# Where the float32 copies of attention's chunks are made: ScalarE against GpSimd

## The chip, the core and the metric

The kernel runs on one core of a Trainium2 chip, in one launch. The metric is the device time of that launch in microseconds (us). A core has five engines that run their own queues of instructions in order and wait for one another by semaphores: TensorE (PE in the profile, with its weight loads as PEld), VectorE (DVE), ScalarE (ACT), GpSimd (POOL) and SyncE (SP, which here only issues transfers).

## The reference, cut to what matters

Causal attention over 2 batches, 12 heads, 448 positions and a head size of 64, then two feed-forward blocks on its result `x` (896 tokens of 768 numbers), all in float32:

```
scores = where(mask, -1e9, q @ k.T / sqrt(64));  p = exp(scores - max) / (sum + 1e-9)
x  = (p @ v)                       # heads side by side: 896 x 768
x  = (x @ w_a * (x @ w_b)) @ w_out # 768 -> 1536 -> 768
h  = x @ w_in;  y = (h * sigmoid(h)) @ w_out2   # 768 -> 2048 -> 768
```

## The kernel before, in words

**Precision.** A float32 product is made of three products of a faster matmul type. Each operand is split: ScalarE (or GpSimd) casts it to a "hi" half, and VectorE subtracts the hi half from the operand to get the "lo" half; TensorE then adds hi·hi, hi·lo and lo·hi. The weights go through the same split in a longer conversion: two instructions on ScalarE (lines 205, 211) and two on VectorE (217, 222) for each of two loads, and then casts (244) and subtractions (248). One pair of weight loads is called a granule.

**Attention** runs over 12 units; a unit is one batch `b` and one chunk of two heads, with batch 0 in units 0 to 5 and batch 1 in units 6 to 11. A unit has four slots, and the program is written slot by slot, 61 slots in all. In a slot TensorE makes the scores of one group of query blocks (lines 552, 556), the transposes (`pt`, line 597) of a group that is 5 slots old, and the products with `v` (`xo`, line 614) of a unit that is 11 slots old. VectorE takes the scores with the mask and the row maxima (`sm`, 564), ScalarE the exponentials (`p`, 568) and the copies of most transposes out of their banks (`ptr`, 697); VectorE makes one `ptr` copy for each unit. The sums of the exponentials are inverted on VectorE (577, 578), and GpSimd multiplies the exponentials by that: the normalisations (581). GpSimd also makes the hi halves of the next unit's q and k (525). The transposes use two banks in turn, so a transpose waits until the copy of an earlier one has emptied its bank. Conversion of the first two granules is spread over slots 8 to 34 and 35 to 52.

**The end of a unit.** When `xo` of a unit is complete, `arrive` (from line 367) puts on ScalarE the cast `xh` (375) and right behind it a float32 copy `xf` (377), and on VectorE the subtraction `xl` (381). The halves are what the feed-forward's matmuls read. The float32 copies are read only by `sums_of` (from 383).

**The sums.** The fast products of the first feed-forward block (Strassen's form over 2 x 2 blocks) need sums and differences of chunks: for each of three pairs of chunks (`c` = 0, 1, 2) four additions `S` on VectorE (390), four casts on ScalarE (395, `p7h`, `p5h`, `p6h`, `p3h`) and four subtractions on VectorE (396). They are handed out one step a slot from slot 44 on, and behind attention one step every three matmuls. A pair can start when its last chunk of batch 1 has arrived: in slots 42, 50 and 58.

**Behind attention** TensorE goes through the granules one after another (line 287 records every such matmul). The first granule's products of batch 0 are mixed into the last slots of attention; the first granule to read the sums, and the first with the fast products, is the third, whose weight tiles are `wa`, `wb`, `wc` and `wd`.

Of the kernel before, what the change touches and what calls it, by code (L numbers as in the profile page):

```python
# [10 lines left out]
F32 = mybir.dt.float32  # L11
# [4 lines left out]
ALU = mybir.AluOpType  # L16
# [17 lines left out]
NQ = 3  # L34
SLOT_HI = 0
SLOT_LO = 2
SUMS0 = 44
SUMS_MM = 3
SPARE = 6
# [18 lines left out]
def fused_kernel(ctx: ExitStack, tc: tile.TileContext, qk, v, w_ab, w_mid, w_in, w_out, out):  # L58
# [14 lines left out]
    nc = tc.nc  # L73
# [45 lines left out]
    A = Ring(slots, [A1], (P, S))  # L119
# [249 lines left out]
    XS, XF = {}, {}  # L369

    def arrive(b, chunk, src):

        hi, lo = A.new(F32R, "xh"), A.new(F32R, "xl")
        XS[chunk, b] = hi, lo
        nc.scalar.copy(out=hi, in_=src)  # L375
        XF[chunk, b] = t = A.new(F32, "xf")
        nc.scalar.copy(out=t, in_=src)  # L377
        c, i = divmod(chunk, 2)
        if (b, i) != (1, 0):
            ACTS[{(0, 0): 1, (0, 1): 2, (1, 1): 4}[b, i]][c] = hi, lo  # L380
        return lambda: nc.vector.tensor_tensor(out=lo, in0=src, in1=hi[:].bitcast(F32), op=ALU.subtract)

    def sums_of(c):


        a11, a12, a21, a22 = (XF.pop((2 * c + i, b)) for b in range(B) for i in range(2))

        def add(name, a, b, op):
            t = A.new(F32, name)
            nc.vector.tensor_tensor(out=t, in0=a, in1=b, op=op)  # L390
            return t

        def halves_of(t, n):
            hi, lo = ACTS[n][c] = A.new(F32R, f"p{n}h"), A.new(F32R, f"p{n}l")
            nc.scalar.copy(out=hi, in_=t)
            return lambda: nc.vector.tensor_tensor(out=lo, in0=t, in1=hi[:].bitcast(F32), op=ALU.subtract)

        s3 = add("S", a11, a21, ALU.subtract)
        yield 2
        rest = halves_of(s3, 7)  # L400
        yield 1
        s1 = add("S", a21, a22, ALU.add)
        rest()
        A.free(a21, a22, s3)
        yield 2
        rest = halves_of(s1, 5)
        yield 1
        s2 = add("S", s1, a11, ALU.subtract)
        rest()
        A.free(s1, a11)  # L410
        yield 2
        rest = halves_of(s2, 6)
        yield 1
        s4 = add("S", a12, s2, ALU.subtract)
        rest()
        A.free(s2, a12)
        yield 2
        rest = halves_of(s4, 3)
        yield 0
        rest()  # L420
        A.free(s4)
# [21 lines left out]
    sums_x = Sums()  # L443
# [20 lines left out]
    with tc.manual_schedule():  # L464

        with ExitStack() as actx:
# [34 lines left out]
            late, now = {}, [0]  # L501
# [3 lines left out]
            def defer(k, prio, fn):  # L505
                late.setdefault(now[0] + k, []).append((prio, fn))
# [13 lines left out]
            def halves_hi(u):  # L520

                for n, src, shape in sources(u):
                    for e in "hl":
                        U[u][n + e] = h_p.tile(shape, F32R, tag=n + e, name=n + e)
                    nc.gpsimd.tensor_scalar(
                        out=U[u][n + "h"], in0=src, scalar1=1.0, scalar2=1.0, op0=ALU.mult, op1=ALU.mult)

            def halves_lo(u):
                for n, src, _ in sources(u):
                    nc.vector.tensor_tensor(  # L530
                        out=U[u][n + "l"], in0=src, in1=U[u][n + "h"].bitcast(F32), op=ALU.subtract)
# [41 lines left out]
            def normalize(u, groups):  # L573
                t = U[u]
                js = [j for i in groups for j in GROUPS[i]]
                cs = slice(COL[js[0]], COL[js[-1]] + 1)
                nc.vector.tensor_scalar_add(out=t["sums"][:, cs], in0=t["sums"][:, cs], scalar1=1e-9)
                nc.vector.reciprocal(out=t["rcp"][:, cs], in_=t["sums"][:, cs])
                for j in js:
                    pj = p_sb[u % 2][j][:, 0:D * (j + 1)]  # L580
                    nc.gpsimd.tensor_scalar(  # L581
                        out=pj, in0=pj, scalar1=t["rcp"][:, COL[j]:COL[j] + 1], scalar2=1.0,
                        op0=ALU.mult, op1=ALU.mult,
                    )
# [20 lines left out]
            def pv(u, kb):  # L605
                t = U[u]
                b, chunk = divmod(u, NP)
                if kb == 0:
                    pool, tag = ps_x, "x"
                    if u % 2:  # L610
                        pool, tag = ps_g[0], "g"
                    t["x"] = pool.tile([P, 512], F32, tag=tag, name="xo")
                for h in range(2):
                    nc.tensor.matmul(  # L614
                        out=t["x"][h * D:(h + 1) * D, kb * P:S], lhsT=t["v"][:, kb, h * D:(h + 1) * D],
                        rhs=t["pt"][:, kb, h, kb * P:S], start=(kb == 0), stop=(kb == NKB - 1),
                    )
                if kb == NKB - 1:
                    defer(1, 0, partial(finish, b, chunk, t["x"][:, 0:S]))
# [3 lines left out]
            def finish(b, chunk, src):  # L623
                tasks.append(arrive(b, chunk, src))
                if b == 1 and chunk % 2:
                    sums_x.gens.append(sums_of(chunk // 2))


            wz = const.tile([P, P], F32, name="wz")
# [38 lines left out]
            for s in range(n_slots):  # L668
# [10 lines left out]
                if i == SLOT_HI and u + 1 < NU:  # L679
                    halves_hi(u + 1)  # L680
                if i == SLOT_LO and u + 1 < NU:
                    halves_lo(u + 1)
# [18 lines left out]
                if 0 <= u < NU and i % 2 == 1:  # L701
                    normalize(u, (i - 1, i))
                if s >= SUMS0:
                    sums_x.step()
# [254 lines left out]
```

## Time and profile before

| what | value |
|---|---|
| three timed runs, median (lowest to highest) | 574.27 us (574.26 to 574.3) |
| the profiled execution's own time | 574.47 us |
| its span, from the first to the last instruction | 572.7 us |
| busy over the span: PE, DVE, ACT, POOL | 559.6, 422.1, 380.3, 72.4 us |
| granted TensorE clock over the span | 1.000 |

The profile is of one execution. What lies between its own time and its span (1.77 us) is outside the instructions. TensorE is busy for 98% of the span, so the places where it is not are few, and they are to be looked at one by one; the other engines' shares are means over stages with different limits.

### The profile page before, as it was taken

How to read it: one execution, taken by the hardware profiler on the slowest of the kernel's cores; microseconds unless marked ns; L12 is line 12 of the kernel's file. 1: busy time of each engine (PE TensorE's matmuls, PEld its weight loads, DVE VectorE, ACT ScalarE, POOL GpSimd, SP SyncE). 2: the span in 40 equal slices, each digit the busy share in tenths (PEclk: the TensorE clock that was granted, in tenths of full speed). 3: DMA queues.
4: the chain of work that ended last, by engine and by line, in shares of the span. 5: the costliest groups of instructions: out<-in, count | busy, mean ns of one | idle time of the engine just before them, and what ended most of it. 6: DMA issues, size and time to landing. Idle time of an engine off the chain costs nothing.

```text
span 572.7 us, 8396 instructions
## 1 busy us (share of the span) xinstructions
PE 559.6 (98%) x2978; PEld 490.4 (86%) x2978; DVE 422.1 (74%) x794; ACT 380.3 (66%) x754; POOL 72.4 (13%) x127
## 2 busy tenths in 40 slices
PE   8999997999999999999999999999999999999997
PEld 6666654799999999999999997899999999999996
DVE  6798897587989898969774769878887798342500
ACT  5989988675666666678654546888876896532601
POOL 6887764000000000000000000000000000000000
PEclk9999999999999999999999999999999999999999
DMA  7354423023333433333333332432324233531501
GB/s 246 115 183 131 121 69 136 1 111 110 111 110 118 160 127 143 116 111 110 112 110 111 110 111 69 152 112 110 111 92 140 81 106 117 169 131 60 175 0 64
DMA packets 18089, 65.41 MB, mean 114 GB/s; under 512 B 2176, under 2 KB 6784, under 8 KB 18048
## 3 DMA queue, kind: packets, MB, share of 16 engines
q1 hardware_dynamic: 18048, 64.89, 33.4%
q8 instruction: 23, 0.38, 0.3%
q14 instruction: 18, 0.15, 0.1%
HBM read 62.13 MB, written 2.75 MB: 113 GB/s over the span
## 4 chain that ended last, share of the span: by engine, by line
PE 89%; DVE 5%; ACT 3%; issue 1%; POOL 1%; DMA 1%; SPq 0%; POOLq 0%; ACTq 0%; DVEq 0%
PE acc L287 79%; PE pt L597 3%; PE xo L614 3%; PE sc L552 2%; PE sc L556 1%; DVE sm L564 1%; DVE wq L222 1%; POOL p L581 1%; ACT ptr L697 1%; DMA k<-qk 1%; ACT p L568 1%; DVE S L337 0%; ACT xf L377 0%; ACT xh L375 0%; DVE wq L217 0%
## 5 line engine op out<-in xcount | busy, mean ns | idle before, releaser
L217 DVE SCALAR_TENSOR_TENSOR wq<-wr 128x768 uint32<-128x768 uint32 (+1 forms) x76 | 66.5, 877 | 27.4 <-ACT wr L211 26.4
L310 ACT COPY s<-acc 128x448 f32<-128x448 f32 x72 | 38.4, 534 | 64.0 <-PE acc L287 63.5
L211 ACT ACTIVATE wr<-wr,wbias 128x768 uint32<-128x768 uint32 (+1 forms) x76 | 69.7, 917 | 0.0
L205 ACT ACTIVATE wr<-wr 128x768 f32<-128x768 f32 (+1 forms) x76 | 63.8, 839 | 3.8 <-DMA wr<-w_out 2.6
L222 DVE SCALAR_TENSOR_TENSOR wq<-wr,wq 128x768 uint32<-128x768 uint32 (+1 forms) x76 | 64.0, 873 | 0.0
L581 POOL TENSOR_SCALAR p<-p,rcp 128x448 f32<-128x448 f32 (+6 forms) x84 | 56.5, 690 | 21.1 <-ACT p L568 15.5
L568 ACT ACTIVATE p<-sm,nmax 128x448 f32<-128x448 f32 (+6 forms) x84 | 42.9, 522 | 10.4 <-DVE nmax L564 9.4
L287 PE MATMUL acc<-th,wgbl 128*128 128x448 f32 x168 | 49.5, 366 | 0.0
L287 PE MATMUL acc<-th,wgbh 128*128 128x448 f32 x168 | 49.4, 366 | 0.0
L287 PE MATMUL acc<-th,wgal 128*128 128x448 f32 x168 | 49.4, 365 | 0.0
L287 PE MATMUL acc<-tl,wgah 128*128 128x448 f32 x168 | 49.4, 366 | 0.0
L287 PE MATMUL acc<-tl,wgbh 128*128 128x448 f32 x168 | 49.4, 365 | 0.0
L287 PE MATMUL acc<-th,wgah 128*128 128x448 f32 x168 | 49.3, 365 | 0.0
L597 PEld LDWEIGHTS pt<-ident,p 128*128 128x128 f32 x192 | 20.2, 140 | 22.4 <-issue 10.8
L597 PE MATMUL pt<-ident,p 128*128 128x128 f32 x192 | 31.0, 285 | 5.5 <-ACT ptr L697 4.5
L564 DVE CUSTOM_DVE_ANT_0 sm<-sc,mask 128x448 f32<-128x448 f32 (+6 forms) x84 | 31.8, 411 | 4.5 <-PE sc L556 4.5
L287 PEld LDWEIGHTS acc<-th,wgbh 128*128 128x128 f32 x168 | 31.5, 188 | 2.9 <-DVE s L754 0.2
L287 PEld LDWEIGHTS acc<-th,wgah 128*128 128x128 f32 x168 | 31.5, 188 | 2.8
L287 PEld LDWEIGHTS acc<-th,wgal 128*128 128x128 f32 x168 | 31.6, 188 | 2.5
L287 PEld LDWEIGHTS acc<-th,wgbl 128*128 128x128 f32 x168 | 31.5, 188 | 2.5
L287 PEld LDWEIGHTS acc<-tl,wgbh 128*128 128x128 f32 x168 | 31.5, 188 | 2.5
L287 PEld LDWEIGHTS acc<-tl,wgah 128*128 128x128 f32 x168 | 31.5, 188 | 2.5
(167 smaller groups left out, 1384.6 us busy)
## 6 DMA issues: line engine op xcount, KB each, us to landing
wr<-w_ab SPq DMA_DIRECT2D x24, 768.0 KB, 5.2
wr<-w_in SPq DMA_DIRECT2D x16, 768.0 KB, 4.5
wr<-w_out SPq DMA_DIRECT2D x24, 512.0 KB, 4.1
wr<-w_mid SPq DMA_DIRECT2D x12, 768.0 KB, 4.5
v<-v SPq DMA_DIRECT2D x12, 256.0 KB, 4.1
q<-qk SPq DMA_DIRECT2D x24, 112.0 KB, 2.9
k<-qk SPq DMA_DIRECT2D x12, 224.0 KB, 3.5
out<-o SPq DMA_DIRECT2D x12, 224.0 KB, 3.9
```

Of the source, the lines that this page charges most:

```text
L205: nc.scalar.activation(out=word(i, 1).bitcast(F32), in_=word(i, 1).bitcast(F32), func=AF.Copy, scale=2.0 ** -112)
L211: nc.scalar.activation(out=word(i, 0), in_=word(i, 0), func=AF.Relu, bias=wbias, scale=2.0 ** -29)
L217: nc.vector.scalar_tensor_tensor(out=xi(i), in0=word(i, 1), scalar=3, in1=word(i, 0), op0=ALU.logical_shift_left, op1=ALU.bitwise_or)
L222: nc.vector.scalar_tensor_tensor(out=xi(i), in0=word(i, 1), scalar=0x80000000, in1=xi(i), op0=ALU.bitwise_and, op1=ALU.bitwise_or)
L287: nc.tensor.matmul(out=acc[:, 0:S], lhsT=w, rhs=a, start=first, stop=last, skip_group_check=True)
L310: nc.scalar.copy(out=t, in_=acc[:, 0:S])
L552: nc.tensor.matmul(out=sc, lhsT=t[a][:, j - BIG].rearrange("p h q -> p (h q)"), rhs=t[k][:, 0:K], start=(n == 0), stop=(n == 2))
L564: nc.vector.tensor_tensor_reduce(out=sm, in0=sc, in1=mask[:, S - K:S], op0=ALU.add, op1=ALU.min, scale=-(D ** -0.5), scalar=3.0e38, accum_ ...
L568: nc.scalar.activation(out=p_sb[u % 2][j][:, 0:K], in_=sm, func=AF.Exp, bias=t["nmax"][:, c:c + 1], scale=-1.0, accum_out=t["sums"][:, c:c ...
L581: nc.gpsimd.tensor_scalar(out=pj, in0=pj, scalar1=t["rcp"][:, COL[j]:COL[j] + 1], scalar2=1.0, op0=ALU.mult, op1=ALU.mult,)
L597: nc.tensor.transpose(out=pt[:, kb].rearrange("p h q -> p (h q)"), in_=p_sb[u % 2][j][:, kb * P:(kb + 1) * P], identity=ident,)
L614: nc.tensor.matmul(out=t["x"][h * D:(h + 1) * D, kb * P:S], lhsT=t["v"][:, kb, h * D:(h + 1) * D], rhs=t["pt"][:, kb, h, kb * P:S], start= ...
```

## The change

`arrive` no longer makes the copy `xf` on ScalarE. A new function `whole` makes it on GpSimd as the sum of the two halves. `finish` puts the four copies of a pair into a later slot: at least slot 49, which follows the last normalisation, and the slot after the pair's arrival where that is later; the pair's sums may start two slots behind that.

```
         hi, lo = A.new(F32R, "xh"), A.new(F32R, "xl")
         XS[chunk, b] = hi, lo
         nc.scalar.copy(out=hi, in_=src)
-        XF[chunk, b] = t = A.new(F32, "xf")
-        nc.scalar.copy(out=t, in_=src)
...
+    def whole(b, chunk):
+
+        hi, lo = XS[chunk, b]
+        XF[chunk, b] = t = A.new(F32, "xf")
+        nc.gpsimd.tensor_tensor(out=t, in0=hi[:].bitcast(F32), in1=lo[:].bitcast(F32), op=ALU.add)
...
             def finish(b, chunk, src):
                 tasks.append(arrive(b, chunk, src))
                 if b == 1 and chunk % 2:
-                    sums_x.gens.append(sums_of(chunk // 2))
+                    for n in range(4):
+                        put_off(partial(whole, n % 2, chunk - 1 + n // 2))
+                    put_off(lambda: sums_x.gens.append(sums_of(chunk // 2)), 2)
+
+            def put_off(fn, k=0):
+                defer(max(0, WHOLE - now[0]) + 1 + k, 9, fn)
```

`WHOLE` is 48. `defer(k, prio, fn)` runs `fn` k slots later. The order of the instructions on TensorE and of the transfers stays the same; it changes on ScalarE, VectorE and GpSimd. Line numbers behind the edit grow by up to 10.

On ScalarE, in the slots in which unit 11's exponentials are made, before:

```order
L568 ACTIVATE p_0_128,sums<-sm,nmax 128x64
L395 CAST p7h<-S 128x448
L244 CAST wgah<-wq 128x768
L375 CAST xh<-xo 128x448
L377 COPY xf<-xo 128x448
L697 COPY ptr<-pt 128x8x64
L568 ACTIVATE p_4_132,sums<-sm,nmax 128x320
```

And the same place with the change:

```order
L573 ACTIVATE p_0_128,sums<-sm,nmax 128x64
L245 CAST wgah<-wq 128x768
L376 CAST xh<-xo 128x448
L707 COPY ptr<-pt 128x8x64
L573 ACTIVATE p_4_132,sums<-sm,nmax 128x320
```

The copy `xf` is gone from in front of `ptr`, as it is in every unit, and the cast `p7h` of the first pair's sums has moved behind the exponentials.

On VectorE, from the last inversion of sums on, before (the numbers tell the buffers apart):

```order
L578 RECIPROCAL rcp_1348<-sums_1346 128x4
L390 TENSOR_TENSOR S_1474<-S_1430,xf_509 128x448
L396 TENSOR_TENSOR p5l_1455<-S_1430,p5h_1454 128x448
L248 TENSOR_TENSOR wgal_1400<-wq_1207,wgah_1399 128x768
L381 TENSOR_TENSOR xl_1521<-xo_1440,xh_1520 128x448
L390 TENSOR_TENSOR S_1527<-xf_624,S_1474 128x448
L396 TENSOR_TENSOR p6l_1507<-S_1474,p6h_1506 128x448
L248 TENSOR_TENSOR wgbl_1510<-wq_1207,wgbh_1509 128x768
L697 COPY ptr_1498<-pt_1539 128x6x64
```

And with the change, where `xf_1474` and `xf_1476` are the first two sums that GpSimd makes:

```order
L583 RECIPROCAL rcp_1332<-sums_1330 128x4
L249 TENSOR_TENSOR wgal_1379<-wq_1193,wgah_1378 128x768
L380 TENSOR_TENSOR xl_1494<-xo_1414,xh_1493 128x448
L249 TENSOR_TENSOR wgbl_1483<-wq_1193,wgbh_1482 128x768
L395 TENSOR_TENSOR S_1522<-xf_1474,xf_1476 128x448
L707 COPY ptr_1466<-pt_1507 128x6x64
L395 TENSOR_TENSOR S_1551<-xf_1476,xf_1480 128x448
```

The first pair's steps have left this stretch, and its first addition `S_1522` now stands in front of the last unit's `ptr` copy.

On GpSimd, the end of the queue with the change:

```order
L586 TENSOR_SCALAR p_4_132<-p_4_132,rcp 128x320
L586 TENSOR_SCALAR p_1_129<-p_1_129,rcp 128x128
L586 TENSOR_SCALAR p_3_131<-p_3_131,rcp 128x256
L586 TENSOR_SCALAR p_2_130<-p_2_130,rcp 128x192
L386 TENSOR_TENSOR xf<-xh,xl 128x448 x12
```

Before, the queue ended with the fourth of these rows; twelve additions now stand behind the last normalisation.

## Rows read from the trace of the kernel before

**Rows 1.** The page: the span, and PE's busy tenths in 40 slices.

```profile
span 572.7 us, 8396 instructions
...
PE   8999997999999999999999999999999999999997
```

**Rows 2.** Stretches: start:end, length, then busy us of PE, PEld, DVE, ACT, POOL.

```profile
60.00:70.00 10.00, 9.51 (x80) 6.51 (x79) 7.99 (x32) 9.90 (x31) 8.36 (x15) 1.00 0.34 100
70.00:80.00 10.00, 8.78 (x69) 6.16 (x71) 8.04 (x26) 8.79 (x30) 6.63 (x9) 1.00 0.05 18
80.00:90.00 10.00, 8.21 (x61) 4.97 (x58) 7.56 (x30) 8.67 (x27) 5.19 (x9) 1.00 0.72 231
90.00:100.00 10.00, 8.48 (x56) 5.42 (x56) 8.84 (x21) 7.61 (x24) 5.21 (x7) 1.00 0.16 63
```

**Rows 3.** Waits of PE, 54 to 115 us: who for whom, total, times, longest.

```profile
PE pt L597 <- ACT ptr L697: 4.5, 6, 1.4
```

**Rows 4.** PE in order of time: start, length, instruction, idle before it.

```profile
80.97 0.63 PE L597 MATMUL pt<-ident,p 128*128 128x128 f32 x4 [0.23 <-ACT ptr L697]
...
89.93 0.63 PE L597 MATMUL pt<-ident,p 128*128 128x128 f32 x4 [1.39 <-ACT ptr L697]
...
93.52 1.13 PE L597 MATMUL pt<-ident,p 128*128 128x128 f32 x8 [0.95 <-ACT ptr L697]
...
96.61 0.63 PE L597 MATMUL pt<-ident,p 128*128 128x128 f32 x4 [0.46 <-ACT ptr L697]
...
102.87 0.97 PE L614 MATMUL xo<-ptr,v 128*64 128x448 f32 x4
```

**Rows 5.** The chain that ended last: start, its share of the path, instruction.

```profile
63.69 0.53 ACT xf L377
...
72.38 0.43 ACT xf L377
...
85.13 0.51 DVE S L390
...
87.25 0.45 ACT p7h L395
...
88.87 0.44 ACT xf L377
...
92.76 0.46 ACT p5h L395
...
93.92 0.47 ACT p6h L395
...
95.55 0.43 ACT xf L377
```

**Rows 6.** Groups of ACT, shapes apart, 0 to 115 us.

```profile
L377 ACT COPY xf<-xo 128x448 f32<-128x448 f32 x12 | 6.6, 548 | 0.0
```

**Rows 7.** Waits of DVE, 0 to 110 us.

```profile
DVE xl L381 <- ACT xf L377: 13.3, 8, 3.7
```

**Rows 8.** Groups of POOL, shapes apart.

```profile
L525 POOL TENSOR_SCALAR kh<-k 128x448 fp32r<-128x448 f32 x11 | 6.3, 570 | 0.0
```

**Rows 9.** The normalisations of line 581: shortest, median and longest in ns.

```profile
L581 POOL TENSOR_SCALAR p<-p,rcp x84: 315/544/1694, 10.0 to 96.0; 128x448 f32<-128x448 f32 x12, 128x384 f32<-128x384 f32 x12, 128x64 f32<-128x64 f32 x12, 128x320 f32<-128x320 f32 x12
```

**Rows 10.** POOL in order of time: its last work.

```profile
93.37 3.07 POOL L581 TENSOR_SCALAR p<-p,rcp 128x320 f32<-128x320 f32 x4 [0.80 <-ACT ptr L697]
```

**Rows 11.** DVE in order of time.

```profile
94.14 1.20 DVE L248 TENSOR_TENSOR wgal<-wq,wgah 128x768 fp32r<-128x768 f32 x1
...
97.63 0.95 DVE L248 TENSOR_TENSOR wgbl<-wq,wgbh 128x768 fp32r<-128x768 f32 x1
...
117.21 1.82 DVE L217 SCALAR_TENSOR_TENSOR wq<-wr 128x768 uint32<-128x768 uint32 x2
```

**Rows 12.** ACT in order of time: the last unit's last copies.

```profile
99.78 0.65 ACT L697 COPY ptr<-pt 128x256 f32<-128x256 f32 x2 [0.43 <-PE pt L597]
```

**Rows 13.** Tile `wal`: its first reader on PE, shortest, median, longest ns, first and last start.

```profile
L287 PE MATMUL acc<-xh,wal x60: 362/368/369, 130.9 to 249.7; 128*128 128x448 f32 x60
```

More of the change, by code (lines that the diff above doesn't have):

```diff
@@ L36 @@
 SLOT_LO = 2
+WHOLE = 48
 SUMS0 = 44
```

## The prediction

> **What bounds the kernel now.** I read the page first. TensorE is full in nearly every slice of the span; the one slice at 7 early on, and the 9s behind it to the last slice, say where to look [rows 1]. So a microsecond is only won where TensorE idles, and it is won for good if it comes before the long full part, because everything behind starts that much sooner.
>
> Next the table of stretches. TensorE idles for 0.49, 1.22, 1.79 and 1.52 us in the four stretches from 60 to 100 us, 5.02 us together [rows 2]; what it idles before that lies in attention's start, ahead of the first `xf`, and behind it every slice is a 9 but the last, the kernel's end [rows 1]. In the same stretches ScalarE is busy for 9.90, 8.79, 8.67 and 7.61 us and VectorE for 7.99, 8.04, 7.56 and 8.84: neither is full all the time, so the idle time is one of order, of who waits for whom.
>
> The list of waits names one pair: transposes wait 6 times for ScalarE's copies `ptr`, 4.5 us in all [rows 3]. TensorE's own rows show four of these gaps with their sizes, 0.23, 1.39, 0.95 and 0.46 us [rows 4]. The chain of waits tells what stands in front of the copy that is late: the float32 copy `xf` four times (63.69, 72.38, 88.87 and 95.55), and from 85 us on also steps of the first pair's sums, `S` on VectorE and the casts `p7h`, `p5h` and `p6h` on ScalarE [rows 5].
>
> **What is removed.** Twelve copies of 548 ns, 6.6 us of ScalarE [rows 6]. One held up the queue by its share of the chain, some 0.43 us. In the first 57 us, four slices, it gets no price here: between its start and there TensorE shows no gap that a copy could close [rows 1].
>
> A second thing goes with them. In the built program the cast `xh` raises no event of its own; the copy behind it raises both. VectorE's `xl` therefore waits for the end of `xf`, which it does not read: 8 times, 13.3 us in all [rows 7]. Most of that is waiting for the cast or for TensorE and stays, but the last 0.43 us of each goes, since the cast now raises the event.
>
> **What is moved.** The sums' steps of the first pair leave slots 44 to 52, where VectorE and ScalarE hold up the transposes, for slots 52 to 60.
>
> The gain, gap by gap; an engine's shift is how much earlier it gets there:
> - near 64.8 us: `xf` at 63.69 is on the chain in front of the late copy: 0.42 of the 0.49 closes.
> - near 73.4 us: `xf` at 72.38 comes on top; ScalarE's shift is 0.85, TensorE's 0.42 already, so 0.42 of that gap closes. Shift of TensorE: 0.84.
> - 80.97: the gap of 0.23 is smaller than one copy and closes. Shift 1.07.
> - 89.93: the chain loses `xf` (0.44), `p7h` (0.45) and `S` (0.51), 1.40, on top of some 0.9 that VectorE has gained since 72 us (the two waits of `xl`). ScalarE's copy is 2.3 earlier, TensorE 1.07: 1.23 of the 1.39 closes. Shift 2.3.
> - 93.52: the exponentials in front of it lose, besides, `p5h` (0.46) and two steps of the sums on VectorE (0.5 each by `S`): ScalarE is 3.7 earlier, so all 0.95 closes. Shift 3.25.
> - 96.61: it loses `xf` (0.43) and `p6h` (0.47): 0.46 closes. Shift 3.71.
>
> So 3.7 of 5.02 us. GpSimd's last normalisation, released by those exponentials, moves up by some 3.2 us, and the transposes that read it had 2 us to spare; no new wait there.
>
> **What is added: twelve additions on GpSimd.** None is in the trace. The nearest row is a one-input GpSimd instruction over the same 448 columns, 570 ns [rows 8]. From below an addition cannot be cheaper than one input read; from above, the longest normalisation took 1,694 ns beside VectorE's work [rows 9]. I take two reads, 1.14 us. Nothing stands behind the additions on GpSimd, so they cost only where VectorE waits for them.
>
> That happens at `S_1522`, which needs the second addition, and behind it in VectorE's queue stands the `ptr` copy for the last unit's product with `v`. In the clock of before: normalisations end at 96.44 [rows 10]; two additions 2.28; between them `wgbl` 0.95 [rows 11]; `S` 0.51; VectorE's copy and ScalarE's behind it, at most 0.65, as two copies [rows 12]; the cast `p7h` 0.45, which now stands in front of the last pair of copies, and that pair 0.65: 101.9. The product starts at 102.87 [rows 4]. A reserve of 0.9, of which 0.5 goes because TensorE moves up by 3.7 and GpSimd by 3.2. I count it as hidden; a GpSimd addition over 1.35 us would begin to show there.
>
> [...]
>
> VectorE and GpSimd also disturb each other: `wgal` took 1.20 us beside a normalisation, `wgbl` 0.95 with GpSimd idle [rows 11]. In the sum I have the additions and VectorE's steps alternate, which for the wait above is the order just used.
>
> [...]
>
> **What becomes late.** The sums of all pairs end later. Behind the last `xl`, 17 of their steps stand on VectorE where there were 11: 6 x 0.51, or 3.1 us. Next in the queue is the third granule's conversion, which began at 117.21 [rows 11], and its `wal` is first read at 130.93 [rows 13]. Of the 13.7 us between, four `wq`, four smaller steps and `wal` take at most 4 x 0.91 + 5 x 0.95 = 8.4. That leaves 5.3, and 2.2 behind the change. Hidden, and if this cover were gone TensorE would wait for `wal`.
>
> **The sum.** 572.7 - 3.7 = 569.0 of span; with the 1.77 outside the span (574.47 - 572.7) 570.8 for this execution. The median of the runs lies 0.2 below the profiled one: 570.6.
>
> **The rivals.**
> - *VectorE takes ScalarE's place.* The weight conversion's long steps stay on VectorE between 73 and 87 us, and if the exponentials wait for them, only the copies' own shares close gaps: 0.42 + 0.42 + 0.23 + 0.44, 1.5 us: 572.8. For it speaks that VectorE is busier than ScalarE in the stretch from 90 us [rows 2]; against it, that the same queue loses its sums' steps there.
> - *Given back.* The gain is made by 100 us and lost again where the sums end late or the last `ptr` copy does: 0.9 and 2.2 us of reserve both overdrawn, about 574.2. For it: both reserves are small. Against it: both rest on prices that I set high.
> - *Slower: GpSimd is the bound.* If an addition takes d and shuts VectorE's two-input steps out meanwhile, twelve additions and as many steps take 12 d + 6.1 from 96.44 on; then come six steps of the last sums (3.1) and the conversion (8.4). `wal` is late by 96.44 + 12 d + 17.6 - 130.93 = 12 d - 16.9. At 1.14 it is not late. From d = 1.72, where this reaches 3.7, the kernel is slower than before; at 2.28, twice my price, by 10.5 - 3.7 = 6.8 us: 581.1. For it: the normalisation of 1,694 ns [rows 9]. Against it: the median there is 544.
>
> **How the numbers follow.** The forecast has 0.66, VectorE as the bound 0.18, given back 0.09, GpSimd as the bound 0.07. A measurement of this kernel can tell about 0.2%, 1.15 us, from no change. The forecast's own range is 569.3 (all 5.02 us closed) to 571.9; VectorE's rival reaches from there to about 573.1. Both are faster by more than 1.15 us, so 0.84 faster, 0.09 the same, 0.07 slower. The range 569.3 to 573.2 leaves out the last two cases and little else.
>
> **What would show it.** In the profile of the changed kernel: TensorE busy for over 9.7 us in each ten from 60 to 100 us; the gaps in front of `pt` gone but for some 0.8 us near 73 us; `xl` waiting for `xh`, and less; the conversion of the third granule still done before TensorE asks for it, with no wait of TensorE behind 100 us; the twelve additions near 1.1 us each. Wrong would be the forecast if TensorE waits for `wal` or for the last `ptr` copy, if an addition takes over 1.4 us, or if the gaps at 90 and 93 us are still there with VectorE as what ends them.

## The result, and the profile after

With the change the kernel takes 578.31 us (median; 577.6 to 578.49 in four runs), beside 574.26 us (574.16 to 574.3) for the kernel before on the same chip: a ratio of 1.0064 [1.0051, 1.0076]. It is slower by 4 us, where 570.6 was forecast. The profiled execution took 578.45 us, with a span of 576.7 us where it was 572.7 [rows 1].

Stretches of the kernel with the change; the columns are those of [rows 2]:

```profile
60.00:70.00 10.00, 10.00 (x85) 7.13 (x86) 8.07 (x31) 9.39 (x30) 7.27 (x13) 1.00 0.37 111
70.00:80.00 10.00, 9.47 (x73) 6.14 (x72) 8.76 (x30) 7.92 (x27) 7.14 (x9) 1.00 0.08 18
80.00:90.00 10.00, 9.06 (x72) 5.65 (x70) 7.08 (x31) 9.13 (x34) 5.41 (x10) 1.00 0.70 250
90.00:100.00 10.00, 9.01 (x59) 6.14 (x55) 6.79 (x5) 2.70 (x7) 9.59 (x10) 1.00 0.08 30
100.00:110.00 10.00, 5.43 (x14) 2.43 (x14) 9.73 (x9) 2.74 (x7) 6.32 (x6) 0.69 0.00 0
```

In each of the first four rows TensorE (the first busy time) is busier than it was. Only the first is over the 9.7 us that the prediction named as its sign: TensorE still waits 0.53 us at 72 us and 0.41 at 87.5 us for `ptr` copies, and the fourth row holds the first microsecond of a new wait. The fifth row is new: TensorE is busy for 5.43 of ten microseconds, at a mean granted clock of 0.69. What it waits for there is in its list of waits, 54 to 150 us:

```profile
PE xo L619 <- ACT ptr L707: 5.6, 1, 5.6
PE pt L602 <- ACT ptr L707: 0.9, 2, 0.5
```

The 4.5 us of [rows 3] have become 0.9, and one wait of 5.6 us has come: the product with `v` waits for a `ptr` copy. The chain that ended last says why that copy is late:

```profile
93.48 2.22 POOL xf L386 x2
...
95.72 7.02 DVE S L395
102.73 0.48 DVE ptr L707
...
103.24 0.27 ACT ptr L707
103.50 0.46 ACT p7h L400
103.97 0.56 ACT ptr L707 x2
...
104.57 1.76 PE xo L619 x4
```

The first addition of the sums, `S_1522`, lasts 7.02 us, where `S` took 0.51 on the chain of before [rows 5]. VectorE's `ptr` copy is queued behind it. What GpSimd does in that time, from its rows in order of time:

```profile
93.45 8.80 POOL L386 TENSOR_TENSOR xf<-xh,xl 128x448 f32<-128x448 f32 x8
103.81 1.13 POOL L386 TENSOR_TENSOR xf<-xh,xl 128x448 f32<-128x448 f32 x1 [1.56 <-DVE S L395]
106.04 2.94 POOL L386 TENSOR_TENSOR xf<-xh,xl 128x448 f32<-128x448 f32 x2 [1.09 <-DVE xl L380]
```

Eight additions run without a break from 93.45 to 102.25. `S` could start at 95.72, when two of them were done, and it ends half a microsecond after the eighth: it did not get its turn for six additions. The run ends only because the ninth addition itself waits for VectorE, for the second `S`, which ends at 103.73. Later rows of VectorE:

```profile
103.12 0.61 DVE L395 TENSOR_TENSOR S<-xf 128x448 f32<-128x448 f32 x1
...
106.42 1.56 DVE L401 TENSOR_TENSOR p5l<-S,p5h 128x448 fp32r<-128x448 f32 x1
107.90 1.55 DVE L395 TENSOR_TENSOR S<-xf,S 128x448 f32<-128x448 f32 x1
```

The second `S` meets no addition and takes 0.61. The two steps from 106.42 on meet the two additions from 106.04 on, and each of them is let in after one addition. So in one and the same execution a step that met a run of eight was held to its end, and steps that met a run of two were not.

The late product has a second cost. TensorE in order of time:

```profile
98.65 0.36 PE L288 MATMUL acc<-xh,wgal 128*128 128x448 f32 x1
104.57 1.76 PE L619 MATMUL xo<-ptr,v 128*64 128x448 f32 x4 [5.55 <-ACT ptr L707]
106.26 0.74 PE L288 MATMUL acc<-xh,wgbh 128*128 128x448 f32 x1
...
111.69 0.47 PE L288 MATMUL acc<-xh,wgah 128*128 128x448 f32 x1
```

And before, the same instructions:

```profile
102.58 0.36 PE L287 MATMUL acc<-xh,wgal 128*128 128x448 f32 x1
...
107.28 0.47 PE L287 MATMUL acc<-xh,wgah 128*128 128x448 f32 x1
```

The clock in that place, with the change (stretch, length, busy us of PE, PEld, DVE, ACT and POOL, then the granted clock):

```profile
104.00:106.00 2.00, 1.43 (x4) 0.30 (x4) 2.00 (x3) 1.41 (x4) 0.94 (x1) 0.50 0.00 0
106.00:108.00 2.00, 2.00 (x7) 1.59 (x6) 2.00 (x3) 0.57 (x1) 1.96 (x2) 0.50 0.00 0
108.00:110.00 2.00, 2.00 (x7) 0.55 (x5) 1.99 (x2) 0.00 (x0) 0.97 (x1) 0.50 0.00 0
110.00:112.00 2.00, 2.00 (x15) 1.48 (x13) 0.00 (x0) 0.19 (x1) 0.00 (x0) 0.85 0.00 0
```

So the account is this. TensorE is 102.58 - 98.65 = 3.93 us earlier when it comes to the wait. From that `acc` to `xo` it takes 5.92 us where it took 102.87 - 102.58 = 0.29 [rows 4], a loss of 5.63. The granted clock is 0.50 for some 6 us behind the idle time, and from `xo` to the last row TensorE takes 111.69 - 104.57 = 7.12 us where it took 4.41: a loss of 2.71. The sum is 4.41 us late at the end of attention (111.69 against 107.28). `wal` is first read at 135.4, 4.5 later than in [rows 13], with no new wait on the way, and the span has grown by 4.0.

### The profile page after: what moved, and what is told of

The parts are those of the page before. It is cut to its first block, busy times and chain, and to the rows that moved or that the text cites. A ratio compares the mean times of both kernels' runs of the same rounds, so it can differ in the third digit from the quotient of the medians.

```text
span 576.7 us, 8389 instructions
## 1 busy us (share of the span) xinstructions
PE 562.0 (97%) x2978; PEld 491.8 (85%) x2978; DVE 432.0 (75%) x794; ACT 375.1 (65%) x742; POOL 85.4 (15%) x139
## 4 chain that ended last, share of the span: by engine, by line
PE 90%; DVE 4%; ACT 2%; POOL 1%; issue 1%; DMA 1%; SPq 0%; POOLq 0%; DVEq 0%; ACTq 0%
PE acc L288 78%; PE pt L602 4%; PE xo L619 3%; PE sc L557 3%; PE sc L561 2%; DVE S L395 1%; POOL p L586 1%; DMA k<-qk 1%; ACT ptr L707 1%; DVE S L338 0%; DVE sm L569 0%; POOL xf L386 0%; SPq L518 0%; DVE wq L218 0%; ACT p L573 0%
## 5 line engine op out<-in xcount | busy, mean ns | idle before, releaser
L586 POOL TENSOR_SCALAR p<-p,rcp 128x448 f32<-128x448 f32 (+6 forms) x84 | 55.2, 672 | 19.5 <-ACT p L573 13.3
L602 PEld LDWEIGHTS pt<-ident,p 128*128 128x128 f32 x192 | 20.2, 141 | 18.6 <-POOL p L586 9.5
L619 PE MATMUL xo<-ptr,v 128*64 128x448 f32 (+3 forms) x192 | 29.2, 404 | 5.8 <-ACT ptr L707 5.8
```

The costliest lines, as they stand in the source:

```text
L586: nc.gpsimd.tensor_scalar(out=pj, in0=pj, scalar1=t["rcp"][:, COL[j]:COL[j] + 1], scalar2=1.0, op0=ALU.mult, op1=ALU.mult,)
L602: nc.tensor.transpose(out=pt[:, kb].rearrange("p h q -> p (h q)"), in_=p_sb[u % 2][j][:, kb * P:(kb + 1) * P], identity=ident,)
L619: nc.tensor.matmul(out=t["x"][h * D:(h + 1) * D, kb * P:S], lhsT=t["v"][:, kb, h * D:(h + 1) * D], rhs=t["pt"][:, kb, h, kb * P:S], start= ...
```

## The experiments

Ratios are to the kernel before on the same chip, whose medians there were 574.26 to 574.86 us. The last two columns are of the one execution that was profiled; the medians are of all executions, three to ten of each kernel here.

| kernel | median us | ratio [95%] | first `S` us | TensorE's wait for the last `ptr` us |
|---|---|---|---|---|
| the change | 578.31 | 1.0064 [1.0051, 1.0076] | 7.02 | 5.6 |
| `ptr` copy first | 576.28 | 1.0023 [1.0008, 1.0039] | 8.15 | none |
| no additions | 570.53 | 0.9932 [0.9917, 0.9947] | 0.85 | none |
| writes instead | 570.62 | 0.9934 [0.9919, 0.9949] | 0.63 | none |
| one input instead of two | 570.25 | 0.9927 [0.991, 0.9944] | 0.97 | none |
| copies kept, sums late | 572.11 | 0.9962 [0.9947, 0.9977] | 0.62 | none |
| copies gone, sums not moved | 571.72 | 0.9954 [0.9939, 0.9969] | 0.59 | none |
| additions on VectorE | 572.08 | 0.9962 [0.9947, 0.9977] | 0.61 | 0.6 |
| a write behind each addition | 572.57 | 0.9972 [0.9961, 0.9983] | 1.59 | 0.2 |
| four additions, then one input | 575.19 | 1.0017 [1.0003, 1.003] | 4.77 | 3.3 |
| four of one input, then additions | 571.26 | 0.9942 [0.9927, 0.9957] | 0.97 | none |
| five additions | 574.85 | 0.9994 [0.9979, 1.0009] | 4.86 | 2.3 |
| five additions, a write behind each | 569.61 | 0.9914 [0.9899, 0.9929] | 1.58 | none |
| a reciprocal before `S` | 578.49 | 1.0068 [1.0045, 1.0091] | 6.76 | 5.5 |
| `S` woken by ScalarE | 573.34 | 0.9998 [0.9965, 1.0032] | 6.00 | 5.6 |

**Is it the additions?** Three kernels replace line 386 of the changed kernel: by nothing (the sums read the hi halves), by a write of a constant, and by a copy of the hi half. So all three leave the lo halves out of the sums, and the second leaves out the hi halves too.

```
-        nc.gpsimd.tensor_tensor(out=t, in0=hi[:].bitcast(F32), in1=lo[:].bitcast(F32), op=ALU.add)
+        XF[chunk, b] = hi                                                    # no additions
+        nc.gpsimd.memset(t, 0.5)                                             # writes instead
+        nc.gpsimd.tensor_scalar(out=t, in0=hi[:].bitcast(F32), scalar1=1.0,  # one input
+                                scalar2=1.0, op0=ALU.mult, op1=ALU.mult)
```

No additions: 

> The changed kernel without the twelve additions on GpSimd; the sums read the hi halves in place of the float32 copies, so the lo halves are left out of them. Same order on the other engines. Lockout theory: S takes 0.6 us, no wait of TensorE near 99 us, clock 1.00, and the time shows the gain by itself: 570.0 to 570.8 us. Rival (the wait comes from the order on VectorE or ScalarE, not from GpSimd): TensorE still waits 4 us or more and the time is 576 us or above.

Writes instead: 

> The changed kernel with each of the twelve additions replaced by a GpSimd memset of the same tile, which reads nothing; the float32 copies hold a constant, so the sums are wrong on values that nothing else depends on for time. By the memset of 448 columns in the trace (0.48 us) the run of eight takes 3.8 us. Lockout by reading: S takes 0.6 us although it runs beside the memsets, no wait of TensorE, 570.0 to 570.8 us. Rival (any run of GpSimd instructions holds it, for instance because the run's end is what releases it): S takes some 3 us, the ptr copy is 2.4 us late and TensorE waits up to 2 us: 571 to 573 us.

One input: 

> The changed kernel with each addition replaced by a one-input GpSimd instruction that copies the hi half (the lo half is left out of the sums), 0.57 us each, a run of eight of 4.6 us. Lockout for the whole run: S starts after the second (1.1 us into the run) and takes 3.4 + 0.5, some 3.9 us; the copy behind it is 3 us early against the changed kernel, TensorE waits 1 to 2.5 us: 571 to 573 us. Rival (lockout for one instruction at a time, VectorE's turn comes after it): S takes at most 1.2 us, no wait of TensorE: 570.0 to 570.8 us.

All three come out near 570.5 us, the time that was forecast for the change. `S` of the kernel with writes, and GpSimd beside it:

```profile
95.16 0.63 DVE L395 TENSOR_TENSOR S<-xf 128x448 f32<-128x448 f32 x1 [1.15 <-POOL xf L386]
```

```profile
94.25 5.04 POOL L386 MEMSET xf<- 128x448 f32 x12
```

The same two of the kernel with one input:

```profile
94.57 0.97 DVE L395 TENSOR_TENSOR S<-xf 128x448 f32<-128x448 f32 x1 [1.39 <-POOL xf L386]
```

```profile
93.45 8.06 POOL L386 TENSOR_SCALAR xf<-xh 128x448 f32<-128x448 f32 x11
```

Beside twelve writes `S` is not held at all. Beside a run of eleven one-input copies it waits out less than one of them (0.73 us each) and gets in. So a run on GpSimd is not enough: in these runs the hold came only where two-input additions stood at its beginning. The one-input copies are also shorter than the additions (0.73 against 1.10 us), and no run parts the number of inputs from the length.

**What the order behind it costs.** One slot more for the sums' start puts the `ptr` copy ahead of `S`:

```
-                    put_off(lambda: sums_x.gens.append(sums_of(chunk // 2)), 2)
+                    put_off(lambda: sums_x.gens.append(sums_of(chunk // 2)), 3)
```

> The changed kernel with the sums started one slot later, so that the last unit's copy ptr stands ahead of the first addition S on VectorE. Theory (lockout): a VectorE instruction with two inputs in SBUF that meets a run of GpSimd additions waits until the whole run is over; the loss came from the ptr copy queued behind it. Then S still takes 5 to 7 us, but TensorE has no wait over 1 us before 110 us, its clock stays at 1.00, and the 3.9 us won by 98.65 us are kept: 570.3 to 571 us. Rival (GpSimd is the bound): the additions hold up VectorE wherever the copy stands, wal becomes late near 127 us, and the time is 573 to 578 us. Rival (the copy was not the cause): TensorE still waits over 4 us near 99 us and the time stays near 578.

The wait near 99 us is gone and the clock of the profiled execution stays at 1.00, but the time is 576.28, and the expected 570.3 to 571 failed: the `ptr` copy was not all that the hold makes late. `S` is now held to the end of nine additions:

```profile
95.73 8.15 DVE L395 TENSOR_TENSOR S<-xf 128x448 f32<-128x448 f32 x1 [1.82 <-POOL xf L386]
```

With it VectorE's whole queue is late, and TensorE pays behind attention, in the waits from 54 to 150 us:

```profile
PE acc L288 <- ACT ga L311: 2.2, 1, 2.2
PE acc L288 <- DVE ga L800: 1.3, 1, 1.3
```

`ga` takes finished products `acc` out of their banks; ScalarE's `ga` copy at 114.39 stands behind a cast `p7h` that had waited for an `S`. The stretches show the wait as TensorE's busy time of 7.80 us from 110 to 120. The rival's time came (573 to 578), though TensorE waits for `ga` and not for `wal`. The order of one copy only decides where the hold is paid. Nine of the ten executions took 575.84 to 576.89 us and one, which was not profiled, 572.24.

**What the two halves of the change are worth.** One kernel keeps ScalarE's copies and only starts the sums later; the other takes the copies out of the kernel before (the sums read hi halves) and leaves the sums in their slots.

```
-                    sums_x.gens.append(sums_of(chunk // 2))                          # copies kept, sums late
+                    defer(max(0, 48 - now[0]) + 3, 9, lambda: sums_x.gens.append(sums_of(chunk // 2)))
-        XF[chunk, b] = t = A.new(F32, "xf")                                          # copies gone
-        nc.scalar.copy(out=t, in_=src)
+        XF[chunk, b] = hi
```

Sums late: 

> The kernel before with only the start of each pair's sums put off to the slots of the changed kernel; the float32 copies stay on ScalarE and GpSimd adds nothing. It parts the gain of 4.2 us that the kernel without additions showed. If the gaps near 89.9 and 93.5 us came from the first pair's sums, as the chain of waits said, most of the gain is here: 571.5 to 572.5 us, and the waits of transposes for ptr fall from 4.5 to about 2 us. Rival (the copies themselves are nearly all of it): 573.5 us or more.

Copies gone: 

> The kernel before with ScalarE's twelve float32 copies taken out and nothing put in their place: the sums keep their slots and read the hi halves alone (left out: the lo halves in the sums). Theory (the gain is made of two parts, copies and the later slots of the sums; the sums kept late with the copies gave -2.4 us and both together -4.0): 572.3 to 573.2 us, about -1.6 us. Rival (the copies carry nearly all of the gain): 570.5 to 571.3 us. Rival (the copies only let VectorE's steps take their place): within 0.5 us of the kernel before.

They win 2.4 and 2.8 us, and both together (no additions) 4.3 on their own chip, less than the sum of 5.2. Both shorten the same waits: TensorE's waits for `ptr` in front of `pt` are 2.6 and 2.4 us there, and 1.0 with both, where they were 4.5. The gain expected for the copies alone, 1.6, was too small by a microsecond.

**Additions on another engine.** The additions on VectorE itself:

```
-        nc.gpsimd.tensor_tensor(out=t, in0=hi[:].bitcast(F32), in1=lo[:].bitcast(F32), op=ALU.add)
+        nc.vector.tensor_tensor(out=t, in0=hi[:].bitcast(F32), in1=lo[:].bitcast(F32), op=ALU.add)
```

> The changed kernel with the twelve additions on VectorE in place of GpSimd, in the same slots. Twelve steps of some 0.54 us on VectorE, eight of them before TensorE leaves attention, where VectorE idled for over 5 us in the kernel without additions. Theory (only the meeting of the two engines cost time): no lockout, the ptr copy 2.2 us later than without additions and still in time: 570.3 to 571.5 us. Rival (VectorE has no room): the third granule's conversion is late by 1 to 3 us: 572 to 574 us.

Twelve more steps on VectorE, the engine that is held, cost some 1.9 us against no additions (2.4 us won on their chip, 4.3 without additions on its own). On GpSimd they cost some 8. No step is held, as expected, but the time is 0.6 us over the expected range, and TensorE waits 0.6 us for the last `ptr` copy, which was expected in time.

**How long the hold lasts.** A write of one column behind each addition, which costs GpSimd 0.1 us and breaks its run:

```
+    gap = const.tile([P, 1], F32, name="gap")
...
+        nc.gpsimd.memset(gap, 0.0)
```

> The changed kernel with a GpSimd memset of one column (about 0.1 us) behind each of the twelve additions. Theory (a run of additions holds VectorE's two-input step because each addition follows the last without a break): the small write breaks the run, S takes at most 1.8 us (one addition and itself), TensorE does not wait near 99 us, 570.3 to 571.5 us. Rival (the hold lasts while any instruction is ready in GpSimd's queue): S still takes 7 us or more and the time stays at 577 to 579 us.

VectorE of that kernel in order of time:

```profile
95.56 1.59 DVE L397 TENSOR_TENSOR S<-xf 128x448 f32<-128x448 f32 x1 [2.57 <-POOL gap L388]
97.08 0.55 DVE L709 COPY ptr<-pt 128x384 f32<-128x384 f32 x1
```

The hold is one addition, and from here on most additions (1.48 to 1.50 us) and most steps (1.56 to 1.59) alternate. That is the alternation that the prediction assumed; here the writes make it. The hold came out as expected, but the time, 572.57 us, is 1.1 over the expected range: the sums still end late, and TensorE waits 1.5 us behind attention (0.7 for `s`, 0.8 for `ga`) and 0.2 for the last `ptr` copy. Then a run with four additions ahead and one-input copies behind:

```
+        if chunk < 2:
             nc.gpsimd.tensor_tensor(...)
+        else:
+            nc.gpsimd.tensor_scalar(...)    # the hi half, as above
```

> The changed kernel with the first pair's four copies as additions and the other eight as one-input copies of the hi half (their lo halves are left out). Theory (only two-input additions in a row hold VectorE): S starts behind the second addition and is held by the third and fourth, 2.2 + 0.6 = 2.8 us, against 7.0; the ptr copy is 4.2 us earlier, TensorE waits 0.5 to 1.5 us: 570.8 to 572 us. Rival (the hold lasts until GpSimd's queue has nothing ready, whatever comes): the run is 4.4 + 2.3 us, S takes 5 us, TensorE waits over 3 us: 573 us or more.

```profile
95.66 4.77 DVE L398 TENSOR_TENSOR S<-xf 128x448 f32<-128x448 f32 x1 [2.54 <-POOL xf L387]
```

```profile
93.39 4.45 POOL L387 TENSOR_TENSOR xf<-xh,xl 128x448 f32<-128x448 f32 x4
97.81 2.16 POOL L389 TENSOR_SCALAR xf<-xh 128x448 f32<-128x448 f32 x4
```

Once held, `S` is held through the one-input copies too, until the run pauses at 99.97; the theory had it let in at 97.84, and its time failed with that. The same the other way round, four copies first (`if chunk >= 2` for the additions):

> The changed kernel with the first four of GpSimd's twelve additions made copies of the hi half (left out: the lo halves of the first pair); eight additions stand behind them. Theory (what counts is the GpSimd instruction that VectorE's step meets: a one-input one lets it in at its end): S starts about 94.6 and takes under 1.2 us, the ptr copy is not late, no wait of TensorE near 99 us; later steps of the sums are held by the run of eight additions for up to 8 us, and TensorE loses little or nothing by that: 572 to 576 us. Rival (VectorE's step is held until GpSimd's queue has nothing ready, whatever stands at its head): S takes 6 us or more, TensorE waits 4 us or more near 99: 576 us or more.

VectorE and GpSimd of that kernel:

```profile
94.74 0.97 DVE L398 TENSOR_TENSOR S<-xf 128x448 f32<-128x448 f32 x1 [1.40 <-POOL xf L389]
95.63 0.55 DVE L710 COPY ptr<-pt 128x384 f32<-128x384 f32 x1
96.17 1.56 DVE L398 TENSOR_TENSOR S<-xf 128x448 f32<-128x448 f32 x1
```

```profile
93.61 2.52 POOL L389 TENSOR_SCALAR xf<-xh 128x448 f32<-128x448 f32 x4
96.10 11.60 POOL L387 TENSOR_TENSOR xf<-xh,xl 128x448 f32<-128x448 f32 x8
```

`S` gets in, as expected. But the second `S` meets a run of eight additions, 0.07 us into its first, and is held for one of them, not for eight; the part of the expectation that had later steps held for up to 8 us failed. From there the additions take 1.45 us each (11.60 for eight) and alternate.

**What decides between hold and alternation?** In four profiles the held step had been woken by the end of an addition; the one let in came straight from other work. Two kernels were to tell that apart: eight reciprocals on VectorE ahead of the first `S`, and five of them followed by a copy on ScalarE that `S` reads.

```
         if c == 0:
+            for _ in range(8):              # 5 in the second kernel
+                nc.vector.reciprocal(out=busy, in_=XS[0, 0][0][:].bitcast(F32))
+            nc.scalar.copy(out=busy, ...)   # second kernel only; S reads busy for a11
```

> The changed kernel with eight extra one-input instructions of 448 columns (reciprocals into a spare tile) on VectorE ahead of the first addition of the sums, so that VectorE comes to it without having waited for GpSimd, in the middle of the run of eight additions. Theory (a step that was woken by the end of a GpSimd addition, and finds the next one running, is held to the end of the run; one that comes straight from other work alternates): the first S takes 0.6 to 1.6 us, the steps behind it 1.0 to 1.6, TensorE waits about 1 us near 99, some 571.5 to 574 us. Rival (any first two-input step that meets a run under way is held to its end): S lasts until about 102 us, TensorE waits 5 to 6 us, 578 us.

> The same with five such instructions and then a copy on ScalarE that the first S has to wait for, in place of GpSimd's first sum (left out: the lo half of one chunk in one sum). VectorE is idle and is woken by ScalarE in the middle of the run. If it is coming out of any wait that lets a step be held: S held to the end of the run at about 102 us and TensorE waits 5 us or more, 577 us or more. If only the wait for GpSimd's own addition does it: S 0.6 to 1.6 us, TensorE waits 0 to 2 us, 571 to 574 us.

Both were inconclusive: a reciprocal of 448 columns takes 2.98 us, so `S` came long after the run of eight. They took 593.1 and 584.79 us, with TensorE waiting 20.2 and 12.1 us for the `ptr` copy queued behind the reciprocals. With one reciprocal each, `S` comes in time:

> The changed kernel with one extra reciprocal on VectorE (2.98 us in the run before, so it ends near 96.1) ahead of the first addition of the sums, which thus meets the run of eight GpSimd additions without a wait. Theory (a step woken by a GpSimd addition's end is held, one that comes straight from other work alternates): S under 1.7 us, TensorE waits under 1 us near 99, 570.5 to 574 us. Rival (any first two-input step that meets a run under way is held to its end): S about 6 us, until 102, TensorE waits 5 to 6 us, about 578 us.

> One such reciprocal and then a copy on ScalarE that the first S waits for in place of GpSimd's first sum, so that it is woken near 96.7, by another engine, in the middle of the run of eight (left out: the lo half of one chunk in one sum). If any wait lets a step be held: S until about 102 us, TensorE waits 5 us or more, 577 us or more. If only the wait for GpSimd's own addition does: S under 1.7 us, TensorE waits 0 to 1.5 us, 570.5 to 574 us.

VectorE and GpSimd of the kernel with one reciprocal, whose run of eight lasts from 94.16 to 102.96:

```profile
93.82 2.94 DVE L406 RECIPROCAL busy<-xh 128x448 f32<-128x448 f32 x1
96.68 6.76 DVE L396 TENSOR_TENSOR S<-xf 128x448 f32<-128x448 f32 x1
```

```profile
94.16 8.80 POOL L387 TENSOR_TENSOR xf<-xh,xl 128x448 f32<-128x448 f32 x8
```

The same two of the kernel in which ScalarE wakes `S`, with the run of eight from 93.72 to 102.54:

```profile
97.03 6.00 DVE L396 TENSOR_TENSOR S<-busy,xf 128x448 f32<-128x448 f32 x1 [0.70 <-ACT busy L407]
```

```profile
93.72 8.82 POOL L387 TENSOR_TENSOR xf<-xh,xl 128x448 f32<-128x448 f32 x8
```

So it is not how VectorE comes to the step: without a wait or out of one for another engine, it is held to the end of the run. The theory of the wait is dropped. The eight timed executions of the last kernel add something: five took 572.8 to 573.56 us and three 578.15 to 578.83, with nothing between. The profiled one is of the upper group, and holds; the distance of 5 us is about the wait of 5.6 that it shows. That the others were let in is not shown, since none of them was profiled, but it would make the hold a matter of the moment at which the step arrives, and not of the program alone. What in that moment decides is open, and so is why the second `S` above was let in, and the two steps of the changed kernel from 106.42 on. One thing sets those apart in the profiles, and no run tests it. There GpSimd had just been held up by VectorE: the four copies ahead of the second `S` took 2.52 us, where four beside a held `S` took 2.16, and the additions at 106.04 began while the `S` from 105.88 ran. The six runs of additions that held a step began with no two-input step of VectorE under way.

**Fewer additions, and a break behind each.** ScalarE keeps the copies of units 0 to 4, 10 and 11, whose waits cost TensorE little, and GpSimd adds for units 5 to 9; once with the write behind each addition and once without.

```
     def arrive(b, chunk, src):
+        if not 5 <= b * NP + chunk < 10:
+            XF[chunk, b] = t = A.new(F32, "xf")
+            nc.scalar.copy(out=t, in_=src)
...
+                        if 5 <= n % 2 * NP + chunk - 1 + n // 2 < 10:
                             put_off(partial(whole, n % 2, chunk - 1 + n // 2))
```

With the write: 

> A version meant to keep the gain: ScalarE keeps the copies of units 0 to 4, 10 and 11, GpSimd adds only for units 5 to 9 (five additions instead of twelve), with a write of one column behind each addition that breaks the run; the sums stay in the later slots. Theory (the hold lasts over a run of additions and a gap ends it): no step of the sums over 1.7 us, TensorE waits under 0.5 us near 99, the copies left on ScalarE cost little: 570.3 to 571.5 us. Rival (the five additions still stop VectorE as one run): S takes over 4 us, 572.5 us or more.

Without: 

> The same five additions without the write behind each. Theory (held for as long as the run lasts): the steps of the sums that meet them are held for the rest of the run, 3 to 5 us, and the wait of TensorE for the last ptr copy near 99 us is 0 to 2 us: 571 to 574 us, over the version with the writes. Rival (the length of the run does not matter, each step is held once for one addition): no step over 1.7 us, the time of the version with the writes.

The run of five without the write holds `S` from its second addition to its end (94.15 + 5.57 = 99.72):

```profile
95.33 4.86 DVE L398 TENSOR_TENSOR S<-xf 128x448 f32<-128x448 f32 x1 [1.45 <-POOL xf L389]
```

With the write it is held for one addition, and the `ptr` copy behind it is in time:

```profile
95.72 1.58 DVE L400 TENSOR_TENSOR S<-xf 128x448 f32<-128x448 f32 x1 [1.44 <-POOL gap L391]
97.23 0.54 DVE L713 COPY ptr<-pt 128x384 f32<-128x384 f32 x1
```

From five writes of one column come 5.2 us. The kernel with them is 0.7 us under the expected range, the one without 0.85 over it: TensorE waits 2.3 us there, and the clock falls behind that in some executions (at the end of this document). At 569.61 us (569.23 to 570.09) this version beats the kernel before by 0.86% [0.71, 1.01], and the changed kernel by more.

## Why the prediction was wrong, step by step

- **What bounds the kernel; what is removed and moved: right in the main.** TensorE comes 3.93 us earlier to the place near 99 us, for 3.7 forecast. The sum is nearer than its terms: of the gap of 1.39 at 89.93 a wait of 0.41 is left (at 87.54), for 0.16 by the forecast, and the others closed as added up or further (near 64.8 us the whole 0.48: the row has 0.53 for the copy there, the prediction took 0.42). Kernels that keep this part and drop the additions land at 570.25 to 570.62, for 570.6 forecast. Of the 13.3 us that `xl` waited for `xf` [rows 7], 6.2 are left up to the last `xl` at 112.4, now for `xh`.
- **The price of an addition: right.** 1.10 us in the run (8.80 for eight), for 1.14, between the bounds of [rows 8] and [rows 9]. Where VectorE's steps come between it is 1.45 to 1.50, over the 1.4 that was to be a sign of error, but those additions cost TensorE nothing that the profile shows.
- **"In the sum I have the additions and VectorE's steps alternate": this step failed.** With it `S` costs 0.51 between additions, the last `ptr` copies are ready at 101.9, and the wait is hidden by a reserve that was to last until an addition took 1.35 us. But the addition's price was not the number that mattered. `S` was held for the rest of the run, 7.02 us, and with it VectorE's `ptr` copy and ScalarE's behind that, the last of which stands behind the cast of `S`, too. The product began at 104.57, where the sum, moved up by GpSimd's 3.2 us, has the copies ready at 98.7. The row of interference that the prediction had, `wgal` with 1.20 us beside a normalisation against 0.95 for `wgbl` [rows 11], is of a one-input GpSimd instruction, and those let VectorE in (0.97 beside the run of eleven). No row of before showed a two-input GpSimd instruction: the alternation was the author's assumption, and the hold was not bounded from above as the price was. With a write behind each addition, where steps and additions do alternate, `S` took 1.59; without, 7.02.
- **The cost of a wait of TensorE: missing from the sum.** The rivals priced a late `ptr` copy by its length alone. 2.71 us came on top from the clock.
- **The slower rival: right in kind, wrong in place and price.** It had VectorE's two-input steps shut out by GpSimd, an assumption that no row of before showed, but one addition at a time, and TensorE waiting for `wal` from 1.72 us an addition on. Here `wal` is in time, and the hold is paid at the last `ptr` copy. Its chance of 0.07 went by the price of an addition, which came out at 1.10; the length of the hold was not in it. "Given back" named the right reserve, the last `ptr` copy's, but not overdrawn by so much.
- **VectorE takes ScalarE's place:** no. Of the gaps near 90 and 93 us [rows 4], 0.41 of 2.34 us is left.

## What to carry to other kernels

Where work moves to GpSimd, count not only its length but how many two-input instructions stand there in a row while VectorE still has two-input steps: here the first of these waited for the whole rest of the row, 7.02 us in all, with everything queued behind it. Cheap breaks helped here: one write of a single column (0.1 us) behind each such instruction won 5.2 us in the kernel with five additions. Handing over only the copies that a waiting engine had paid for won another 3.0 against twelve with the writes. And a stretch in which TensorE waits is priced with the clock that may follow, which cost another 2.7 us on 5.55 here.

## What the runs showed of the hardware

- A run of back-to-back two-input GpSimd additions can hold one two-input VectorE instruction to its end: 7.02, 8.15, 4.86, 6.76 and 6.00 us in five profiles, where it takes 0.61 alone. It does not always: a step that met a run of eight, and others that met runs of two, were let in after one addition (1.55 to 1.57 us), and what decides is open. In the profile with four additions ahead of one-input GpSimd instructions it was held through those too (4.77).
- A VectorE reciprocal over 448 float32 columns takes 2.94 to 2.98 us, where an addition of two such tiles takes 0.61.
- The granted clock is not settled by the length of one wait alone. It fell to 0.50 behind waits of 5.55 and 2.31 us, and stayed at 1.00 behind one of 3.31 in the profiled execution of the kernel with four additions. That execution is one of three at a mean clock of 1.000, which took 573.52 to 573.59 us; the other seven had 0.994 or 0.997 and took 574.99 to 576.77. With five additions four executions at 1.000 took 572.84 to 573.20 us and six at 0.997 took 574.78 to 576.39. So within one kernel the clock may fall or not, and 1.4 to 3.6 us go with it; the waits of the executions that were not profiled are not known. In the profiled one of those six, behind the wait of 2.31:

```profile
102.00:104.00 2.00, 1.97 (x7) 1.18 (x8) 1.21 (x4) 1.31 (x3) 0.00 (x0) 0.71 0.00 0
104.00:106.00 2.00, 2.00 (x7) 1.14 (x7) 1.64 (x4) 0.56 (x1) 0.00 (x0) 0.50 0.00 0
```

And in the profiled execution of the kernel with four additions, TensorE's first rows behind the wait of 3.31, whose `acc` takes 0.47 us and not the 0.74 of the changed kernel:

```profile
102.27 0.97 PE L622 MATMUL xo<-ptr,v 128*64 128x448 f32 x4 [3.31 <-ACT ptr L710]
103.17 0.47 PE L288 MATMUL acc<-xh,wgbh 128*128 128x448 f32 x1
```
